# Attention output with tokens on partitions: exponentials as the stationary operand, 65 moving columns

## The chip, the cores and the metric

The kernel runs on one core of a Trainium2 chip. The metric is the device time of one execution in microseconds (us), the median of several runs. The engines are named as the profile names them: PE is TensorE (PEld its weight loads), ACT is ScalarE, DVE is VectorE, POOL is GpSimd, SP is SyncE, which here only issues DMA transfers.

## The reference

Attention with an exponential feature map, without softmax over keys, and then a feed-forward block with g = h cos h:

```python
def phi(x):
    proj = np.einsum('bhsd,df->bhsf', x, w_phi)
    proj = proj - np.max(np.abs(proj), axis=-1, keepdims=True)
    return np.concatenate([np.exp(proj), np.exp(-proj)], axis=-1)
q_p, k_p = (phi(q), phi(k))
kv = np.einsum('bhsf,bhsd->bhfd', k_p, v)
z = np.sum(k_p, axis=2)
num = np.einsum('bhsf,bhfd->bhsd', q_p, kv)
den = np.einsum('bhsf,bhf->bhs', q_p, z)[..., None] + 1e-06
attn = num / den
...
x = attn.transpose(0, 2, 1, 3).reshape(B * S, H * D)
h = x @ w_in
out = (h * np.cos(h)) @ w_out
```

There are 8 batches of 8 heads, 576 tokens (S), 64 columns a head (D), 128 features (256 after phi). The feed-forward block takes 4608 tokens, 512 columns in, 2048 hidden, 512 out. All is float32.

## The kernel before

**Attention** works in 32 units u, each a batch and a pair of heads (j = 0, 1). A unit loads q and k with head columns on partitions (qr, kr) and v with tokens on partitions (vmain, vtail, with a 65th column of ones). PE projects them (q_mm, k_mm), DVE takes the largest absolute value, it is subtracted, and ACT takes exponentials: ek with tokens on partitions, eq with features on partitions, `[128, 2, 576]` for each head, one half for each sign. kv_mm (line 666) multiplies ek by v: for each of 4 token slots, 2 heads, 2 signs and 2 halves of 64 features, 64 stationary columns of ek against the 65 moving columns of v. So one PSUM bank holds kv and, in each 65th column, z. kv_out copies them to SBUF: kv (line 680) and z, repeated 32 times (line 681).

The attention output then comes with head columns on partitions and tokens moving. z_mm (line 705) forms the denominators: the 32 copies of z are stationary, 288 tokens move, 8 matmuls into four 32-row groups of one bank. n_mm (line 715) forms the numerators: 64 columns of kv stationary, 512 tokens moving, and the 64 tail tokens into the free end of the bank of z_mm. Meanwhile invert (DVE, lines 721 to 725) reduces the 32 equal rows with a transposing reduction, adds 1e-6 and takes reciprocals; spread (ACT, line 732) moves four blocks of 32 partitions; turn (DVE, line 736) repeats them over 576 columns by transposing 32-blocks; times (DVE, line 740) multiplies numerators by them, the tail first. store (SP, line 744) writes the 128 x 576 result to the scratch tensor xs in DRAM, one DMA, 2304 bytes a row.

**The feed-forward block** reads xs back as x_raw, 512 tokens (a chunk c) at a time, splits it in high and low float32r parts (x_high on ACT, x_low on DVE), and passes pairs of 128-wide hidden blocks through mm1 (line 905 for the first three chunks, line 857 in a seven-product scheme for the others), cosine, and mm2 (lines 954 to 956). Chunks 0 to 2 are visited several times (visits 0 to 8) while the weights are being converted by ACT and DVE; chunks 3 to 8 once each (visits 9 to 14) with weights reloaded from DRAM. A chunk of 512 tokens needs the four units of each batch it touches: chunk 0 units 0 to 3, chunk 1 units 0 to 7, chunk 2 units 4 to 11.

**Order.** Each piece of work is a `Step` with an engine, a planned cost, the steps it depends on, and the buffers it takes and uses. The table `ORDER` lists all steps, 3572 of them, and is the program order on each engine: engines run their steps in that order and wait on semaphores. `plan()` only gives out the 8 PSUM banks along it. The costs given to `Step` do not act at run time. SBUF buffers come in rings (`rings`: for instance rb=2, kv=2, x_raw=4). `K_SUMS` names the units in which PE subtracts the maxima of k itself (k_sub, line 610), so that ACT can take exponentials of 512 columns at once (line 619); in the other units ACT does it with a bias per 128 columns (line 622), and DVE makes the negative of the maxima (line 605).

Of the kernel before, what the change touches and what calls it, by code (L numbers as in the profile page):

```python
# [17 lines left out]
P = 128  # L18
# [7 lines left out]
def phi_attention_then_cos_ffn(ctx: ExitStack, tc: tile.TileContext, qT, kT, vS, vT, w_phi, w_in, w_out, out):  # L26
# [41 lines left out]
    class Step:  # L68
# [16 lines left out]
    SHAPE = dict(mm1="full", mm2="full", one="full", k_mm="upper", k_end="full", q_end="full", k_sub="full", kv_mm="left", n_mm="left", z_mm="quarter", q_mm="upper")  # L85
    ORDER = [
# [237 lines left out]
    def bank(b):  # L324
        return banks[b.slot]
# [26 lines left out]

    GROUP = 3
    Q_DVE = range(0)
    K_SUMS = range(8)
    WARM = 7
    WHOLE = 8  # L360
    W_POOL = ()
    PLAIN = 9
    NP = NFT // 2
    HC = CT // 2
# [123 lines left out]

    stored, quotient, chain_v = {}, {}, {}

    def attention(u):
        d = {}
# [579 lines left out]
```

## Time and profile before

| | us |
|---|---|
| runs of the kernel before | 1080.25, 1080.84, 1082.85 (median 1080.84) |
| the profiled execution | 1081.13 |
| its span, first to last instruction | 1079.0 |
| PE busy | 1061.1 |
| ACT busy | 833.2 |
| DVE busy | 781.3 |
| POOL busy | 145.2 |

A row of the profile's groups reads: line, engine, operation, output<-inputs, shapes, xcount, then busy time in all, mean ns of one, and the idle time of that engine just before them with what ended it. Matmuls are pipelined and their ends are modelled, so the cost of one in a stream is read from the distance of two starts. A float32 matmul counts as two instructions, a float32r one as one. A row of the waits reads: who waited <- for whom: total us, times, longest us.

### The profile page before, as it was taken

What the parts mean: (1) busy time and instruction counts of PE and PEld (TensorE: products, weight loads), DVE (VectorE), ACT (ScalarE), POOL (GpSimd) and SP (SyncE); (2) the same over time, 40 slices, a digit from 0 to 9 for tenths busy, and PEclk for the clock granted to TensorE, in tenths of its full rate; (3) what the DMA queues carried; (4) which work ended last, traced back from release to release, by engine and by line L of the source; (5) the groups of instructions that cost most, each with busy time, mean ns of one, the idle gap of its engine ahead of it and who ended that gap; (6) DMA issues with size and microseconds to landing.
All of it is one profiled execution on the core that took longest, in us unless ns stands there. A gap on an engine that the chain in (4) does not pass through costs nothing.

```text
span 1079.0 us, 21627 instructions
## 1 busy us (share of the span) xinstructions
PE 1061.1 (98%) x8462; PEld 850.1 (79%) x8462; DVE 781.3 (72%) x1337; ACT 833.2 (77%) x1794; POOL 145.2 (13%) x175
## 2 busy tenths in 40 slices
PE   9999999999999999999999999999999999999998
PEld 6565666778878877888877977877788888998996
DVE  6999989899989977666776657675676556455544
ACT  6999998898886789777789778898788565454533
POOL 4424222100100210101311110211101100000000
PEclk9999999999999999999999999999999999999999
DMA  7564383566656643795356563457244743761952
GB/s 236 157 195 139 125 293 116 211 240 222 219 228 248 201 171 123 244 376 198 103 180 208 198 223 127 144 213 271 108 162 160 244 148 119 259 230 43 326 207 78
DMA packets 97477, 207.51 MB, mean 192 GB/s; under 512 B 43744, under 2 KB 50016, under 8 KB 91488
## 3 DMA queue, kind: packets, MB, share of 16 engines
q1 hardware_dynamic: 97216, 206.07, 55.4%
q8 instruction: 66, 1.08, 0.4%
q14 instruction: 35, 0.29, 0.1%
q10 hardware_dynamic: 160, 0.07, 0.0%
HBM read 155.78 MB, written 50.33 MB: 191 GB/s over the span
## 4 chain that ended last, share of the span: by engine, by line
PE 81%; ACT 8%; DVE 7%; DMA 1%; issue 1%; SPq 1%; ACTq 0%; DVEq 0%
PE bank L857 21%; PE bank L954 11%; PE bank L955 11%; PE bank L956 11%; PE bank L905 10%; PE bank L715 4%; PE bank L666 4%; PE bank L705 2%; ACT ek L622 2%; PE bank L566 2%; PE bank L520 2%; ACT eq L628 1%; PE bank L672 1%; DVE mk L602 1%; PE bank L610 1%
## 5 line engine op out<-in xcount | busy, mean ns | idle before, releaser
L954 PE MATMUL bank<-wo,gh 128*128 128x512 f32 x576 | 228.7, 397 | 0.0
L955 PE MATMUL bank<-wo,gh 128*128 128x512 f32 x576 | 225.7, 392 | 0.0
L956 PE MATMUL bank<-wo,gl 128*128 128x512 f32 x576 | 224.6, 390 | 0.9 <-DVE gl L54 0.9
L869 ACT ACTIVATE hs<-bank 128x256 f32<-128x256 f32 x192 | 70.6, 384 | 97.6 <-PE bank L857 87.4
L931 DVE SCALAR_TENSOR_TENSOR g<-g,hs 128x512 f32<-128x512 int32 x144 | 102.7, 725 | 43.2 <-ACT g L927 34.3
L956 PEld LDWEIGHTS bank<-wo,gl 128*128 128x128 f32 x576 | 108.2, 188 | 25.0 <-DVE gl L54 1.3
L938 DVE TENSOR_TENSOR g<-hs,g 128x512 f32<-128x512 f32 x144 | 101.2, 709 | 36.8 <-ACT g L935 36.3
L54 DVE TENSOR_TENSOR gl<-g,gh 128x512 fp32r<-128x512 f32 x144 | 100.5, 703 | 37.8 <-ACT gh L49 37.2
L954 PEld LDWEIGHTS bank<-wo,gh 128*128 128x128 f32 x576 | 108.6, 189 | 24.3 <-issue 4.2
L559 POOL TENSOR_TENSOR pq<-pq,bq 128x576 f32<-128x576 f32 x64 | 101.4, 1604 | 178.4 <-DVE bq L555 164.4
L857 PE MATMUL bank<-xh_t,wi 128*128 128x256 f32 x768 | 124.3, 284 | 0.0
L935 ACT ACTIVATE g<-g,halfpi 128x512 f32<-128x512 f32 x144 | 101.9, 719 | 27.3 <-DVE g L931 26.6
L955 PEld LDWEIGHTS bank<-wo,gh 128*128 128x128 f32 x576 | 108.7, 189 | 17.2
L857 PEld LDWEIGHTS bank<-xh_t,wi 128*128 128x128 f32 x768 | 110.5, 190 | 11.1 <-issue 1.7
L551 POOL COPY m<-m 32x36 f32<-32x36 f32 x96 | 42.4, 441 | 530.4 <-DVE m L546 526.5
L49 ACT ACTIVATE gh<-g 128x512 fp32r<-128x512 f32 x144 | 91.1, 635 | 25.9 <-DVE g L938 14.1
L857 PE MATMUL bank<-xh_b,wi 128*128 128x256 f32 x576 | 93.4, 284 | 0.0
L905 PE MATMUL bank<-xh_b,wi 128*128 128x512 f32 x288 | 82.9, 396 | 4.5 <-ACT ek L622 3.0
L857 PEld LDWEIGHTS bank<-xh_b,wi 128*128 128x128 f32 x576 | 81.6, 191 | 6.2 <-DVE g L938 1.5
L628 ACT ACTIVATE eq<-pq 128x576 f32<-128x576 f32 x128 | 80.3, 694 | 5.3 <-PE bank L715 3.8
L857 PE MATMUL bank<-xl_t,wi 128*128 128x256 f32 x384 | 77.3, 283 | 0.0
L666 PEld LDWEIGHTS bank<-vmain,ek 128*64 128x64 f32 x2048 | 63.5, 138 | 15.4 <-issue 8.1
(98 smaller groups left out, 1928.3 us busy)
## 6 DMA issues: line engine op xcount, KB each, us to landing
wi<-wi_parts SPq DMA_DIRECT2D x30, 1792.0 KB, 8.2
wo<-wo_parts SPq DMA_DIRECT2D x30, 1024.0 KB, 6.1
wi_parts<-wi SPq DMA_DIRECT2D x8, 2048.0 KB, 9.5
x_raw<-xs SPq DMA_DIRECT2D x60, 256.0 KB, 5.0
qr<-qT SPq DMA_DIRECT2D x32, 320.0 KB, 4.9
kr<-kT SPq DMA_DIRECT2D x32, 320.0 KB, 4.9
xs<-rb SPq DMA_DIRECT2D x32, 288.0 KB, 3.2
vmain<-vS SPq DMA_DIRECT2D x32, 256.0 KB, 4.5
```

What stands on the lines that cost most here:

```text
L49: ACT.activation(out=out, in_=in_, func=AF.Copy, scale=1.0)
L54: eng.tensor_tensor(out=out, in0=in_, in1=hi.bitcast(F32), op=ALU.subtract)
L559: qeng.tensor_tensor(out=d["pq"][:, c], in0=d["pq"][:, c], in1=d["bq"][:, c], op=ALU.subtract)
L666: PE.matmul(out=acc[c:c + 64, n, i, :], lhsT=e[:, s, P * n + c:P * n + c + 64], rhs=vmain[u % 2][:, s, i, :], start=(s == 0 and i == 0 and ...
L857: PE.matmul(out=out, lhsT=w[:, part, block, j * P:(j + 1) * P], rhs=d[x, name][:, j * HC:(j + 1) * HC], start=start and k == 0, stop=k == ...
L905: PE.matmul(out=bank(b), lhsT=w[:, part, 2 * r + kt // 2, kt % 2 * P:(kt % 2 + 1) * P], rhs=d[x, BLOCKS[kt]], start=(k == 0), stop=(k == 3 ...
L931: DVE.scalar_tensor_tensor(out=g, in0=g.bitcast(I32), scalar=-TWO_PI, in1=m["hs", r], op0=ALU.mult, op1=ALU.add)
L935: ACT.activation(out=n["g"], in_=n["g"], func=AF.Sin, bias=halfpi, scale=1.0)
L938: DVE.tensor_tensor(out=n["g"], in0=m["hs", r], in1=n["g"], op=ALU.mult)
L954: PE.matmul(out=a, lhsT=gh[:, t], rhs=w[:, 0, r], start=first, stop=False)
L955: PE.matmul(out=a, lhsT=gh[:, t], rhs=w[:, 1, r], start=False, stop=False)
L956: PE.matmul(out=a, lhsT=gl[:, t], rhs=w[:, 0, r], start=False, stop=last)
```

## The change

The output is formed with tokens on partitions. x_mm takes the place of z_mm and n_mm: 64 columns (tokens) of eq are stationary, and the 65 columns of kv with z, as kv_mm left them, move. It is two steps with a bank each: 16 matmuls for token slots 0 and 1, and 16 for slots 2 and 3 with 4 for the tail. Numerators and their denominator then lie in the same row, so invert reads the 65th columns, adds 1e-6 and takes reciprocals, and times multiplies each row by its own, in pieces of 32 columns placed so that a 32-block transposition (turn, now at the end) brings head columns onto partitions. The result lies in four groups of 32 partitions, and store writes it with eight DMAs. The host permutes the columns of q to suit. kv_out is one copy of 65 columns per group, and z's copy, spread, and the 32 copies of z are gone. `K_SUMS` goes from 8 units to 7. The order table is a new one, with 3538 steps; three planned costs (w.sums, mul, kv_out) change, which act only on how such a table is made.

```diff
-    SHAPE = dict(..., kv_mm="left", n_mm="left", z_mm="quarter", q_mm="upper")
+    SHAPE = dict(..., kv_mm="left", x_mm="left", q_mm="upper")
     ORDER = [
...
-    rings.update(..., eq=3, kv=2, rb=2,
+    rings.update(..., eq=3, kv=2, rb=1, xt=2,
...
-    K_SUMS = range(8)
+    K_SUMS = range(7)
...
         def kv_out():
-            acc = d["acc"][:, 0:260].rearrange("p (g c) -> p g c", c=65)
-            kv = d["kv"] = new("kv", [P, 4, 64], F32, "kv")
-            z = d["z"] = new("kv", [P, 4, 32], F32, "z", "z")
-            ACT.activation(out=kv, in_=acc[:, :, 0:64], func=AF.Copy, scale=1.0)
-            ACT.activation(out=z, in_=acc[:, :, 64:65].broadcast_to([P, 4, 32]), func=AF.Copy, scale=1.0)
+            kv = d["kv"] = new("kv", [P, 4, 65], F32, "kv")
+            ACT.activation(out=kv, in_=d["acc"][:, 0:260].rearrange("p (g c) -> p g c", c=65), func=AF.Copy, scale=1.0)
...
+        def x_mm(i):
+            ps = d["xps", i] = bank(xb[i])
+            started = set()
+            for t in (2 * i, 2 * i + 1):
+                for j in range(2):
+                    for n in range(2):
+                        for h in range(2):
+                            c = P * t + 64 * h
+                            g = 2 * (t - 2 * i) + j
+                            PE.matmul(out=ps[64 * h:64 * h + 64, 65 * g:65 * g + 65], lhsT=d["eq", j][:, n, c:c + 64],
+                                      rhs=d["kv"][:, 2 * n + j, :], start=h not in started, stop=n == 1, skip_group_check=True)
+                            started.add(h)
+            if i == 1:
                 for n in range(2):
                     for j in range(2):
+                        PE.matmul(out=ps[64 * j:64 * j + 64, 260:325], lhsT=d["eq", j][:, n, CT:S], rhs=d["kv"][:, 2 * n + j, :],
+                                  start=False, stop=n == 1, skip_group_check=True)
 
         def invert():
+            dn = d["dn"] = new("rb", [P, 9], F32, "dn", "dn")
+            for i, (g, n) in enumerate(((0, 4), (4, 5))):
+                DVE.tensor_scalar(out=dn[:, g:g + n], in0=d["xps", i][:, 0:65 * n].rearrange("p (g c) -> p g c", c=65)[:, :, 64], scalar1=1e-6,
+                                  scalar2=None, op0=ALU.add)
+            DVE.reciprocal(out=dn, in_=dn)
+
+        def times(i):
+            if i == 0:
+                d["rb"] = new("rb", [P, S], F32, "rb")
+            n = 4 + i
+            x = d["xps", i][:, 0:65 * n].rearrange("p (g c) -> p g c", c=65)[:, :, 0:64]
+            f = d["dn"][:, 4 * i:4 * i + n].unsqueeze(2).broadcast_to([P, n, 64])
+            for t in range(2):
+                o = d["rb"][:, 0:CT].rearrange("p (j e t b) -> p t j e b", j=2, e=2, t=NSLOT)[:, 2 * i + t]
+                y, z = (v[:, 2 * t:2 * t + 2, :].rearrange("p j (e b) -> p j e b", e=2) for v in (x, f))
+                DVE.tensor_tensor(out=o, in0=y, in1=z, op=ALU.mult)
+            if i == 1:
+                DVE.tensor_tensor(out=d["rb"][:, CT:S], in0=x[:, 4], in1=f[:, 4], op=ALU.mult)
 
         def turn():
+            d["xt"] = new("xt", [P, S], F32, "xt")
+            DVE.transpose(out=d["xt"], in_=d["rb"])
 
         def store():
             bt, hp = u // NHP, u % NHP
-            SP.dma_start(out=xs[hp * P:(hp + 1) * P, bt * S:(bt + 1) * S], in_=d["rb"])
+            x = d["xt"]
+            rows = xs[hp * P:(hp + 1) * P, bt * S:(bt + 1) * S].rearrange("(q p) t -> p q t", p=32)
+            for a in range(4):
+                r = slice(32 * a, 32 * a + 32)
+                SP.dma_start(out=rows[:, :, P * a:P * a + P], in_=x[r, 0:CT].rearrange("p (q t) -> p q t", q=4))
+            for a in range(4):
+                r, j, h = slice(32 * a, 32 * a + 32), a // 2, a % 2
+                SP.dma_start(out=rows[:, 2 * j:2 * j + 2, CT + 32 * h:CT + 32 * h + 32], in_=x[r, CT:S].rearrange("p (q t) -> p q t", q=2))
+
+        xb = [Buf("bank", "a"), Buf("bank", "a")]
+        mms = []
+        for i in range(2):
+            mms.append(Step("PE", 0.94 if i == 0 else 1.18, lambda i=i: x_mm(i), [ko] + eqs, take=[xb[i]], use=[b["kv"]] + eqb, kind=phase + "x_mm"))
+        dv = Step("DVE", 0.45, invert, mms, take=[b["rb"]], use=xb, kind=phase + "invert")
+        outs = [Step("DVE", 0.4 if i == 0 else 0.5, lambda i=i: times(i), [mms[i], dv], use=[xb[i], b["rb"]], kind=phase + "times") for i in range(2)]
+        outs[1].deps.append(outs[0])
+        tn = Step("DVE", 0.69, turn, outs, take=[b["xt"]], use=[b["rb"]], kind=phase + "turn")
+        stored[u] = Step("SP", 1.6, store, [tn], use=[b["xt"]], kind=phase + "store")
...
     qT, kT = blocks(q), blocks(k)
+    w = n * P
+    qT[..., :w] = qT[..., :w].reshape(NU, 2 * D, 4, n, 32).swapaxes(2, 3).reshape(NU, 2 * D, w)
```

More of the change, by code (lines that the diff above doesn't have):

```diff
@@ L84, in phi_attention_then_cos_ffn @@
     SWITCH = dict(e=1.3, s=1.3, full=0.23, left=0.147, quarter=0.138, upper=0.195)
-    SHAPE = dict(mm1="full", mm2="full", one="full", k_mm="upper", k_end="full", q_end="full", k_sub="full", kv_mm="left", n_mm="left", z_mm="quarter", q_mm="upper")
+    SHAPE = dict(mm1="full", mm2="full", one="full", k_mm="upper", k_end="full", q_end="full", k_sub="full", kv_mm="left", x_mm="left", q_mm="upper")
     ORDER = [
[199 rows of a table removed]
[197 rows of a table added]
     ]
@@ L309, in phi_attention_then_cos_ffn @@
     ps = ctx.enter_context(tc.tile_pool(name="ps", bufs=1, space=PSUM))
-    rings.update(wi=3, wo=3, v=2, kr=2, qr=2, pq=2, bq=1, pk=4, pk_t=2, ek=2, ek_t=2, eq=3, kv=2, rb=2,
+    rings.update(wi=3, wo=3, v=2, kr=2, qr=2, pq=2, bq=1, pk=4, pk_t=2, ek=2, ek_t=2, eq=3, kv=2, rb=1, xt=2,
                  x_raw=4, hs=4, g=3, gh=3, gl=3, o=2, w_raw=1, w_t=1)
@@ L468, in convert @@
         if kind == "wi":
-            s8 = Step(name, 1.32 * slow, sums, [s4, s6], use=[t], port=True, kind="w.sums")
+            s8 = Step(name, 1.71 * slow, sums, [s4, s6], use=[t], port=True, kind="w.sums")
             s9 = Step("ACT", 0.95, sums_high, [s8], use=[t, slot], kind="w.sums_high")
@@ L485, in reload @@
         w_ready[me] = [Step("SP", 5.6 if kind == "wi" else 3.2, load, w_stored[me], take=[slot], kind="r.load")]
-    stored, quotient, chain_v = {}, {}, {}
+    stored, chain_v = {}, {}
     def attention(u):
@@ L497, in attention @@
         qname, qeng, qcost = ("DVE", DVE, 0.77) if u in Q_DVE else ("POOL", POOL, 1.5)
-        b = {k: Buf(k) for k in ("kr", "qr", "v", "pq", "bq", "kv", "rb")}
+        b = {k: Buf(k) for k in ("kr", "qr", "v", "pq", "bq", "kv", "rb", "xt")}
         def load():
@@ L691, in attention @@
                         kind=phase + "kv_mm")
-        ko = Step("ACT", 0.45, kv_out, [last], use=[acc, b["kv"]], kind=phase + "kv_out")
-        N0 = CT
-        cut = [slice(0, N0), slice(N0, S)]
-        def z_mm():
-            d["zps"] = ps = bank(zps)[:, 0:HALF]
-            d["nps", 0], d["nps", 1] = bank(nps)[:, 0:N0], bank(zps)[:, HALF:HALF + S - N0]
-            for n in range(2):
-                for hf in range(2):
-                    for j in range(2):
-                        g = 2 * j + hf
-                        PE.matmul(out=ps[32 * g:32 * g + 32], lhsT=d["z"][:, 2 * n + j, :],
-                                  rhs=d["eq", j][:, n, hf * HALF:(hf + 1) * HALF], start=(n == 0), stop=(n == 1),
-                                  skip_group_check=True)
@@ L709, in n_mm @@
-        def n_mm():
-            for hf in (1, 0):
+        ko = Step("ACT", 0.27, kv_out, [last], use=[acc, b["kv"]], kind=phase + "kv_out")
+        def x_mm(i):
[11 more added lines that the diff above has]
+            if i == 1:
@@ L713, in n_mm @@
                 for n in range(2):
                     for j in range(2):
-                        PE.matmul(out=d["nps", hf][64 * j:64 * j + 64], lhsT=d["kv"][:, 2 * n + j, :],
-                                  rhs=d["eq", j][:, n, cut[hf]], start=(n == 0 and hf == 0), stop=(n == 1),
-                                  skip_group_check=True)
+                        PE.matmul(out=ps[64 * j:64 * j + 64, 260:325], lhsT=d["eq", j][:, n, CT:S], rhs=d["kv"][:, 2 * n + j, :],
+                                  start=False, stop=n == 1, skip_group_check=True)
@@ L719, in invert @@
         def invert():
-            dn = d["dn"] = new("rb", [P, NJ], F32, "dn", "dn")
-            DVE.tensor_reduce(out=dn, in_=d["zps"].rearrange("p (j t) -> p j t", t=32), axis=AX.X, op=ALU.max,
-                              apply_transpose=True)
-            DVE.tensor_scalar(out=dn, in0=dn, scalar1=1e-6, scalar2=None, op0=ALU.add)
-            d1 = d["d1"] = new("rb", [P, 2 * NJ], F32, "d1", "d1")
-            DVE.reciprocal(out=d1.rearrange("p (h b) -> p h b", h=2), in_=dn.unsqueeze(1).broadcast_to([P, 2, NJ]))
@@ L727, in spread @@
-        def spread():
-            for q in range(4):
-                c = slice((1 - q % 2) * NJ, (2 - q % 2) * NJ)
-                r, o = 32 * q, 32 * (q ^ 1)
-                ACT.activation(out=d["d1"][r:r + 32, c], in_=d["d1"][o:o + 32, c], func=AF.Copy, scale=1.0)
-        def turn():
-            d["rb"] = new("rb", [P, S], F32, "rb")
-            DVE.transpose(out=d["rb"], in_=d["d1"].unsqueeze(2).broadcast_to([P, 2 * NJ, 32]))
-        def times(hf):
-            rb = d["rb"][:, cut[hf]]
-            DVE.tensor_tensor(out=rb, in0=d["nps", hf], in1=rb, op=ALU.mult)
+            dn = d["dn"] = new("rb", [P, 9], F32, "dn", "dn")
@@ L742, in store @@
+        def turn():
+            d["xt"] = new("xt", [P, S], F32, "xt")
+            DVE.transpose(out=d["xt"], in_=d["rb"])
         def store():
             bt, hp = u // NHP, u % NHP
-            SP.dma_start(out=xs[hp * P:(hp + 1) * P, bt * S:(bt + 1) * S], in_=d["rb"])
-        zps, nps = Buf("bank", "a"), Buf("bank", "a")
-        zm = Step("PE", 0.97, z_mm, [ko] + eqs, take=[zps], use=[b["kv"]] + eqb, kind=phase + "z_mm")
-        dv = Step("DVE", 0.9, invert, [zm], take=[b["rb"]], use=[zps], port=True, kind=phase + "invert")
@@ L749, in attention @@
-        dv = Step("ACT", 0.9, spread, [dv], use=[b["rb"]], kind=phase + "spread")
-        dv = Step("DVE", 0.7, turn, [dv], use=[b["rb"]], kind=phase + "turn")
-        mm = Step("PE", 1.94, n_mm, [zm], take=[nps], use=[zps, b["kv"]] + eqb, kind=phase + "n_mm")
-        outs = [Step("DVE", 0.61 if ps is nps else 0.14, lambda hf=hf: times(hf), [mm, dv], use=[ps, b["rb"]], kind=phase + "times") for hf, ps in ((1, zps), (0, nps))]
-        stored[u] = Step("SP", 0.9, store, outs, use=[b["rb"]], kind=phase + "store")
@@ L754, in attention @@
-        d["b"] = b["rb"]
-        quotient[u] = d
+            x = d["xt"]
[6 more added lines that the diff above has]
+                SP.dma_start(out=rows[:, 2 * j:2 * j + 2, CT + 32 * h:CT + 32 * h + 32], in_=x[r, CT:S].rearrange("p (q t) -> p q t", q=2))
@@ L859, in product, with mul @@
                             k += 1
-                def mul(bank_b, half, block, name, start, deps, cost=0.685, wi=wi, product=product):
+                def mul(bank_b, half, block, name, start, deps, cost=0.72, wi=wi, product=product):
                     return Step("PE", cost, lambda: product(bank_b, half, block, name, start), [ready[name]] + w_ready[wi] + deps,
```

396 rows, old and new, of the table ORDER are left out of this document.

## The prediction

> **What bounds the kernel now.** I read the page's head and busy table first, then the 40 slices, the idle time of TensorE (PE), stretches of the span, and last the in-stream cost of the steps that go.
>
> ```profile
> span 1079.0 us, 21627 instructions
> ...
> PE 1061.1 (98%) x8462; PEld 850.1 (79%) x8462; DVE 781.3 (72%) x1337; ACT 833.2 (77%) x1794; POOL 145.2 (13%) x175
> ...
> PEclk9999999999999999999999999999999999999999
> ```
>
> ```profile
> 0.00:30.00 30.00, 27.81 (x294) 18.07 (x294) 21.30 (x40) 21.30 (x44) 11.70 (x28) 1.00 0.68 212
> 30.00:330.00 300.00, 293.37 (x2508) 211.08 (x2506) 276.10 (x451) 270.38 (x571) 58.59 (x62) 1.00 0.58 195
> 330.00:870.00 540.00, 535.92 (x4412) 439.25 (x4411) 371.27 (x662) 436.88 (x970) 74.89 (x85) 1.00 0.57 197
> 870.00:1079.00 209.00, 204.03 (x1260) 181.69 (x1252) 112.64 (x187) 104.64 (x212) 0.00 (x0) 1.00 0.48 174
> ```
>
> The columns of the second are stretch, length, busy time of PE, PEld, DVE, ACT and POOL, granted clock, DMA share and GB/s. PE is busy 98% at full clock everywhere. From 330 us on nothing else is near: DVE has 371.27 of 540 us. But from 30 to 330 us three engines are nearly full together: PE 98%, DVE 92%, ACT 90%. So a microsecond taken off PE is worth a microsecond late, and early only as far as DVE and ACT can follow. The profiled execution took 1081.13 us, the span of 1079.0 and 2.1 us around it; the median of the runs is 1080.84, the same within its spread, so I sum against 1081.1.
>
> **PE: the two products that go, and the one that comes.** This is one unit of attention in the PE's own order of time (start, length, what; the length of the last includes the drain, so starts are what counts):
>
> ```profile
> 823.99 0.40 PE L857 MATMUL bank<-xl_b,wi 128*128 128x256 f32 x2
> 824.31 1.18 PE L705 MATMUL bank<-eq,z 128*32 128x288 f32 x16
> 825.42 2.17 PE L715 MATMUL bank<-eq,kv 128*64 128x64 f32 x16
> 827.42 2.04 PE L666 MATMUL bank<-vmain,ek 128*64 128x65 f32 x64
> 829.29 0.61 PE L672 MATMUL bank<-vtail,ek 128*64 128x130 f32 x8
> 829.83 0.50 PE L954 MATMUL bank<-wo,gh 128*128 128x512 f32 x1
> 830.17 0.39 PE L955 MATMUL bank<-wo,gh 128*128 128x512 f32 x1
> 830.40 0.40 PE L956 MATMUL bank<-wo,gl 128*128 128x512 f32 x1
> ```
>
> z_mm (L705) holds PE 825.42 - 824.31 = 1.11 us, n_mm (L715) 827.42 - 825.42 = 2.00: 3.11 us a unit go. The new product has 16 + 20 = 36 matmuls, 64 stationary columns of exponentials against 65 moving ones, alternating between the two output halves. That is the very form of kv_mm (L666), whose 32 matmuls show as 64 instructions (float32 counts twice) in 829.29 - 827.42 = 1.87 us, 29.2 ns each, weight loads included. So 72 x 29.2 ns = 2.10 us come, 1.01 less a unit, **32 x 1.01 = 32.3 us**.
>
> The clearest objection is the weight load, since the wide operand now is the stationary one.
>
> ```profile
> L666 PEld LDWEIGHTS bank<-vmain,ek 128*64 128x64 f32 x2048 | 63.5, 138 | 15.4 <-issue 8.1 <-ACT pq L531 1.4 <-ACT ek L619 1.0
> L666 PE MATMUL bank<-vmain,ek 128*64 128x65 f32 x2048 | 66.6, 223 | 0.0
> ```
>
> One load takes 138 ns, but 2048 of them occupy only 63.5 us, 31 ns each: they overlap, four at a time. I take the 29.2 ns. The Trainium skill, "TensorE: Matmul & The Clock Gate", section "LDWEIGHTS (loading the stationary operand)", prices a load by its columns alone, columns / 1.2 ns; an estimate by that page is 64 / 1.2 = 53 ns a load, 72 loads 3.8 us a unit, 0.7 us more than the 3.11 that go, 23 us slower in all. The trace disagrees with its use as a rate here: 64 loads and matmuls took 1.87 us, not 3.4.
>
> **Changes of shape.** By the order tables, neighbouring PE steps differ in stationary shape 187 times before and 152 after (the 32 visits to a 32-column shape go). At 823.99 two matmuls of 118 ns end at 824.23 and z_mm starts at 824.31, 0.08 us lost; at 829.83 the next start comes after 0.34 us instead of 0.23, 0.11 lost. 35 x 0.09 = **3.2 us** off PE (0 where a change hides behind a wait).
>
> **A wait inside the old pair.** The tail of n_mm lies in z_mm's bank, so it waits until DVE has read the sums.
>
> ```profile
> PE bank L715 <- DVE dn L721: 3.8, 6, 0.7
> PEld bank L715 <- DVE dn L721: 7.8, 7, 1.2
> ```
> ```profile
> 869.21 1.18 PE L705 MATMUL bank<-eq,z 128*32 128x288 f32 x16
> 871.00 2.17 PE L715 MATMUL bank<-eq,kv 128*64 128x64 f32 x16 [0.61 <-DVE dn L721]
> ```
>
> There 871.00 - 869.21 = 1.79 instead of 1.11, 0.68 us lost, 6 or 7 times: 4 to 5. The halves of the new product have a bank each and nothing between them waits for DVE: **4.5 us** off. Both start, as z_mm did, behind kv_out on ACT and the exponentials; that wait stays.
>
> **K_SUMS 8 to 7.** Unit 7's two maxima are no longer subtracted by PE (L610) but as a bias of ACT's exponentials (L622 in place of L619).
>
> ```profile
> L610 PE MATMUL bank<-mk,minus 128*128 128x512 f32 x32 | 16.3, 612 | 0.2 <-DVE mk L602 0.2
> L622 ACT ACTIVATE ek<-bank,mk 128x128 f32<-128x128 f32 x224 | 70.0, 429 | 0.0
> L619 ACT ACTIVATE ek<-bank 128x512 f32<-128x512 f32 x32 | 17.2, 608 | 1.5 <-PE bank L666 1.0 <-PE bank L610 0.5
> ```
>
> PE: 16.3 us over 16 steps, so two steps are **2.0 us** less. ACT: 16 x 0.43 for 4 x 0.61, 4.4 us more, once, hidden or not by the sum for ACT below.
>
> PE in all: 32.3 + 3.2 + 4.5 + 2.0 = 42.0 us less, 1039 if every microsecond counts.
>
> **DVE.** Rows of what goes, and the nearest rows of what comes:
>
> ```profile
> L721 DVE TRANSPOSE_TENSOR_REDUCE dn<-bank 128x9 f32<-128x288 f32 x32 | 15.2, 477 | 17.3 <-PE bank L705 11.2 <-PE bank L715 6.1
> L725 DVE RECIPROCAL d<-dn 128x18 f32<-128x18 f32 x32 | 8.5, 266 | 1.1
> L723 DVE TENSOR_SCALAR dn<-dn 128x9 f32<-128x9 f32 x32 | 7.9, 245 | 1.1
> L736 DVE STREAM_TRANSPOSE rb<-d 128x576 f32<-128x576 f32 x32 | 24.6, 768 | 5.7 <-ACT d L732 5.5
> L740 DVE TENSOR_TENSOR rb<-bank,rb 128x512 f32<-128x512 f32 x32 | 21.8, 681 | 1.6 <-PE bank L715 1.1
> L740 DVE TENSOR_TENSOR rb<-bank,rb 128x64 f32<-128x64 f32 x32 | 6.9, 215 | 0.5
> L888 DVE TENSOR_TENSOR hs<-bank,hs 128x256 f32<-128x256 f32 x48 | 20.3, 422 | 54.2 <-PE bank L857 43.9 <-ACT gh L49 3.6 <-ACT g L927 3.0
> ```
>
> Gone per unit: 0.477 + 0.245 + 0.266 + 0.768 + 0.681 + 0.215 = 2.65 us. Coming: two small additions from the banks (0.245 each), a reciprocal of 9 (at most 0.266), four products of 128 columns, one of 64, and a turn of 576. A product of 128 columns lies between 0.215 (64) and 0.422 (256); along that line 0.284. Sum 0.49 + 0.27 + 4 x 0.284 + 0.215 + 0.768 = 2.88, **0.23 more**, between -0.05 (four at 0.215) and +0.78 (four at 0.422, if the strided 32-column pieces are slow). That is 3 us over the 14 units of the early stretch; late it is hidden by DVE's idle third.
>
> **ACT** loses the copy of z and the four spreads:
>
> ```profile
> L732 ACT ACTIVATE d<-d 32x9 f32<-32x9 f32 x128 | 26.7, 209 | 8.6 <-DVE d L725 7.0
> L681 ACT ACTIVATE z<-bank 128x128 f32<-128x128 f32 x32 | 8.9, 280 | 0.0
> ```
>
> 4 x 0.209 + 0.280 = 1.12 us a unit, 36 us in all, 15.6 in the early stretch against the 4.4 above: ACT falls from 270 to 259 us of work there. It is off the bound late; early it is what lets PE move up.
>
> **What the early stretch gives back.** Units 1 to 14 lie between 30 and 330 us (z_mm's 224 instructions there, 16 a unit):
>
> ```profile
> 30.00:330.00 300.00, 17.18 (x224) 5.87 (x224) 1.00 0.58 195
> ```
>
> PE would save 14 x 1.11 + 2.0 + about 2 of the waits = 19.5 us there, and the stretch would last 280.5. DVE has 276.1 + 3 = 279 us to do in it, 99.6%: too much. The new table puts 357 DVE steps ahead of unit 14's product where the old has 362; five steps of some 0.7 us leave 276. Between DVE's 92% of now and 100% I take 96%, which is an estimate: 276 / 0.96 = 288, so 12.5 of the 19.5 us are got and **7 are lost**, as new idle time of PE. Ends: 0 lost, or all 19.5.
>
> **SP and DMA.** One store of 128 rows becomes eight issues, in 32-partition pieces. They go through SP's queue in order, in front of loads.
>
> ```profile
> 509.84 0.32 SPq L744 DMA_DIRECT2D xs<-rb  x1
> 510.25 0.39 SPq L785 DMA_DIRECT2D x_raw<-xs  x1
> 510.73 0.45 SPq L483 DMA_DIRECT2D wo<-wo_parts  x1
> 511.24 0.56 SPq L507 DMA_DIRECT2D vmain<-vS  x1
> ```
> ```profile
> SPq L483 <- PE bank L857: 170.7, 27, 22.8
> ...
> SPq L783 <- DMA xs<-rb: 20.1, 8, 3.8
> ```
>
> An issue takes 0.3 to 0.6 us, so eight take about 4.4 us instead of 0.33; the step's planned cost rises only from 0.9 to 1.6. Queued behind are the next units' q, k and v and the rows of the chunk (x_raw), whose reader is ACT (x_high), then PE. Late, SP itself mostly waits for PE to give up weight buffers (170.7 us, first row), so four more microseconds find room there: nothing. Early, three chunks begin on stores just made (the second row: SP waits up to 3.8 us for a store to land before it issues x_raw). If each came 4 us late, 12 us; if the loads have that lead, 0. I take **2**. The bytes are the same and the DMA share stands at 0.48 to 0.68 in the stretches above: nothing.
>
> **Sum.** 1081.1 - 42.0 + 7 + 2 = 1048.
>
> **Rivals.**
> 1. *All of PE's saving counts* because the new order fills the early stretch: 1039. For it: ACT has 11 us less to do there. Against: DVE would need 99.6%.
> 2. *The early stretch gives nothing*, since DVE, not PE, sets its end: 1081.1 - 42.0 + 19.5 = 1059; with slow strided products (+0.55 us for 14 units) up to 1066. For it: DVE 92% busy already. Against: idle 8%, and ACT, the second brake, is relieved.
> 3. *Slower: SP's queue becomes the bound.* Each store holds it 4.1 us longer. It decides from the point where a unit costs PE over 1.3 us of waiting (42.0 / 32). If units 0 to 11, whose stores the first three chunks and the next units' loads wait for, each passed the full 4.1 us on, and the early saving were gone as well: 1059 + 49 = 1108. For it: in-order queue, stores sit right ahead of loads. Against: units are some 10 to 15 us apart there.
> 4. *Slower: the weight loads run one after the other.* Alternating 64-column loads at 138 ns, 72 of them, is 9.9 us a unit, 6.8 more, in all 1081 + 218 = 1299; the point is 3.11 us / 72 = 43 ns a load. Against it stands the same form at 29.2 ns.
> 5. *No change*: gains on PE and new waits cancel, 1081.
>
> **How the numbers follow.** The forecast (1042 to 1056) has 0.48, rival 1 (1036 to 1042) 0.15, rival 2 (1056 to 1066) 0.22, something between 1066 and 1078 0.04, rival 5 0.04, rival 3 0.05, rival 4 0.02. So faster by over 0.3% (about what a measurement of this kernel can tell from no change) 0.89, within 0.04, slower 0.07. The range 1038 to 1064 leaves out rivals 3 to 5, the gap and the outer ends of 1 and 2, under 0.2.
>
> **What would show it.** After: 72 new PE instructions per unit in about 2.1 us, some 29 ns each, and no 128x288 form; PE's busy time near 1020 us, its waits for DVE's dn gone; DVE busy over 94% in the first 300 us, with new PE idle time there that names DVE or ACT; the store's eight issues over 4 us. I am wrong if the new product takes over 2.5 us a unit, if the products of 128 columns take over 0.4 us, or if PE waits long for x_raw or for q and k early.

## The result and the profile after

The changed kernel takes 1054.09 us (median; 1052.74 to 1056.54) against 1081.45 before, ratio 0.9749 with an interval of 0.9727 to 0.9771: 27 us faster. The profiled execution took 1054.31 us with a span of 1052.6. The forecast was 1048 within 1038 to 1064.

Head and busy times of the page of the changed kernel:

```profile
span 1052.6 us, 24383 instructions
...
PE 1032.3 (98%) x9738; PEld 882.6 (84%) x9738; DVE 758.5 (72%) x1435; ACT 794.7 (76%) x1640; POOL 131.0 (12%) x175
```

PE's busy time fell by 28.8 us (1061.1 to 1032.3; the prediction named "near 1020" as a sign) and its share stayed 98%: it is still the bound. The stretches (length, busy time and count of PE, PEld, DVE, ACT, POOL, granted clock, DMA share, GB/s):

```profile
0.00:30.00 30.00, 28.53 (x342) 19.96 (x344) 21.09 (x46) 21.64 (x42) 10.19 (x28) 1.00 0.70 210
30.00:330.00 300.00, 288.28 (x3087) 230.84 (x3087) 274.32 (x508) 262.76 (x522) 54.70 (x65) 0.99 0.61 196
330.00:870.00 540.00, 537.71 (x5227) 472.31 (x5226) 368.09 (x732) 421.37 (x899) 66.11 (x82) 1.00 0.60 203
```

From 30 to 330 us PE was idle 300 - 288.28 = 11.7 us; before it was 6.6. Late, 2.3 of 540; before 4.1. So late PE waits for next to nothing, and the early stretch gave something back, as forecast. But DVE is at 274 of 300 us there, 91%, not at 96%: something else held it up. One unit of the new product late, in order of time:

```profile
763.34 2.09 PE L699 MATMUL bank<-kv,eq 128*64 128x65 f32 x64
765.25 0.40 PE L705 MATMUL bank<-kv,eq 128*64 128x65 f32 x8
765.49 2.04 PE L664 MATMUL bank<-vmain,ek 128*64 128x65 f32 x64
767.35 0.61 PE L670 MATMUL bank<-vtail,ek 128*64 128x130 f32 x8
```

765.49 - 763.34 = 2.15 us for 72 instructions, 29.9 ns each, where 2.10 was forecast; kv_mm right behind it takes 1.86 for its 64, 29.1 ns. So loading the exponentials as the stationary operand adds nothing to the 29 ns that an instruction of this form takes.

The DVE rows that answer to those forecast:

```profile
L724 DVE TENSOR_TENSOR rb<-bank,dn 128x128 f32<-128x128 f32 x128 | 29.3, 279 | 0.4
L730 DVE STREAM_TRANSPOSE xt<-rb 128x576 f32<-128x576 f32 x32 | 24.7, 771 | 0.7 <-DMA xs<-xt 0.2 <-issue 0.2
L713 DVE RECIPROCAL dn<-dn 128x9 f32<-128x9 f32 x32 | 6.9, 215 | 1.1
L726 DVE TENSOR_TENSOR rb<-bank,dn 128x64 f32<-128x64 f32 x32 | 6.7, 211 | 0.0
L711 DVE TENSOR_SCALAR dn<-bank 128x5 f32<-128x5 f32 x32 | 4.9, 154 | 9.3 <-PE bank L705 5.9 <-ACT hs L865 3.4
L711 DVE TENSOR_SCALAR dn<-bank 128x4 f32<-128x4 f32 x32 | 4.8, 148 | 7.4 <-PE bank L699 7.4
```

4 x 0.279 + 0.771 + 0.215 + 0.211 + 0.154 + 0.148 = 2.62 us a unit against the 2.65 that went: DVE is not charged at all (0.23 more was forecast; the small additions and the reciprocal make most of the difference).

What does stand out is SP's queue and what waits behind it. The first fence is the queue from 61 to 70 us, the second PE's waits and the third ACT's waits for transfers, of the changed kernel (the fourth is ACT's row of the kernel before):

```profile
61.27 0.43 SPq L502 DMA_DIRECT2D kr<-kT  x1
62.49 3.73 SPq L738 DMA_DIRECT2D xs<-xt  x4
66.26 1.85 SPq L741 DMA_DIRECT2D xs<-xt  x4
68.22 0.37 SPq L501 DMA_DIRECT2D qr<-qT  x1
68.69 0.38 SPq L502 DMA_DIRECT2D kr<-kT  x1
69.15 0.39 SPq L779 DMA_DIRECT2D x_raw<-xs  x1
```
```profile
PE bank L901 <- ACT ek L620: 4.1, 3, 1.7
PE bank L564 <- DMA kr<-kT: 1.9, 1, 1.9
```
```profile
ACT xh_t L49 <- DMA x_raw<-xs: 6.9, 3, 2.4
ACT xh_b L49 <- DMA x_raw<-xs: 4.2, 2, 2.7
```
```profile
ACT xh_b L49 <- DMA x_raw<-xs: 1.0, 1, 1.0
```

One store holds SP's queue from 62.49 to 68.11, 5.6 us, and x_raw is issued behind it, at 69.15. ACT then waits 11.1 us in all for x_raw, 8.4 of them before 330 us; before, it was 1.0. ACT works in order, so what stands behind x_high waits too, and then mm1 on PE (line 901). This is the same place in the timeline of ACT and PE; between the two lines ACT computes ek until 76.63, and mm1 waits for that:

```profile
73.44 0.63 ACT L49 ACTIVATE xh_t<-x_raw 128x512 fp32r<-128x512 f32 x1 [2.28 <-DMA x_raw<-xs]
76.67 1.35 PE L901 MATMUL bank<-xh_b,wi 128*128 128x512 f32 x3 [1.58 <-ACT ek L620]
```

PE's wait for kr (line 564) is another matter: that kr was issued at 61.27, ahead of this store and behind the one before, and landed 5.9 us later. What made it late is open.

### The profile page after: what moved, and what is told of

It reads as the page before. It is cut to its first block, busy times and chain, and to the rows that moved or that the text cites. A ratio compares the mean times of both kernels' runs of the same rounds, so it can differ in the third digit from the quotient of the medians.

```text
span 1052.6 us, 24383 instructions
## 1 busy us (share of the span) xinstructions
PE 1032.3 (98%) x9738; PEld 882.6 (84%) x9738; DVE 758.5 (72%) x1435; ACT 794.7 (76%) x1640; POOL 131.0 (12%) x175
## 4 chain that ended last, share of the span: by engine, by line
PE 78%; DVE 7%; DMA 6%; ACT 5%; SPq 2%; issue 1%; POOL 0%; ACTq 0%; DVEq 0%; POOLq 0%
PE bank L853 22%; PE bank L950 11%; PE bank L951 11%; PE bank L952 11%; PE bank L901 10%; PE bank L699 3%; PE bank L664 3%; PE bank L564 2%; PE bank L518 2%; ACT ek L620 2%; DMA xs<-xt 1%; DMA x_raw<-xs 1%; DMA vmain<-vS 1%; SPq L738 1%; SPq L741 1%
## 5 line engine op out<-in xcount | busy, mean ns | idle before, releaser
L927 DVE SCALAR_TENSOR_TENSOR g<-g,hs 128x512 f32<-128x512 int32 x144 | 99.3, 697 | 54.7 <-ACT g L923 45.9
L54 DVE TENSOR_TENSOR gl<-g,gh 128x512 fp32r<-128x512 f32 x144 | 97.7, 683 | 34.7 <-ACT gh L49 33.8
L557 POOL TENSOR_TENSOR pq<-pq,bq 128x576 f32<-128x576 f32 x64 | 97.7, 1548 | 191.1 <-DVE bq L553 151.1
L549 POOL COPY m<-m 32x36 f32<-32x36 f32 x96 | 31.9, 332 | 501.7 <-DVE m L544 499.0
L620 ACT ACTIVATE ek<-bank,lk 128x128 f32<-128x128 f32 x232 | 71.4, 407 | 5.5 <-DVE lk L603 3.5
```

Of the source, the lines that this page charges most:

```text
L54: eng.tensor_tensor(out=out, in0=in_, in1=hi.bitcast(F32), op=ALU.subtract)
L557: qeng.tensor_tensor(out=d["pq"][:, c], in0=d["pq"][:, c], in1=d["bq"][:, c], op=ALU.subtract)
L620: ACT.activation(out=e[:, g, s * P:(s + 1) * P], in_=pk[:, g, :], func=AF.Exp, scale=1.0 - 2.0 * s, bias=d["lk" if s == 0 else "mk", i][:, ...
L927: DVE.scalar_tensor_tensor(out=g, in0=g.bitcast(I32), scalar=-TWO_PI, in1=m["hs", r], op0=ALU.mult, op1=ALU.add)
```

## The experiments

Differences are taken between the ratios to the kernel before, times 1082 us; the interval of a difference is put together from both (root of the sum of squares).

**What the eight stores cost.** `one_store`, the unit's result as it lies, in one DMA:

```diff
-            for a in range(4): ... SP.dma_start(out=rows[:, :, P * a:P * a + P], ...)
-            for a in range(4): ... SP.dma_start(out=rows[:, 2 * j:2 * j + 2, ...], ...)
+            SP.dma_start(out=xs[hp * P:(hp + 1) * P, bt * S:(bt + 1) * S], in_=d["xt"])
```

> The changed kernel, with the store of each unit as one DMA of 128 rows again instead of eight (the rows then land in other places than the reference has them; bytes the same). Theory A, that the eight issues in SP's queue hold up the loads of x_raw and of q and k in the first 330 us: 5 to 8 us less, 1046 to 1049. Rival B, that DVE and ACT are too full there and the queue costs nothing: 0 to 2 less, 1052 to 1054. ACT's wait for x_raw before 330 us (8.4 us in the changed kernel) should fall to about 1 either way.

Measured 1045.95 us, ratio 0.9661 (0.9641 to 0.9681): 9.5 us less than the changed kernel, give or take 3.2. That is theory A, a little above its range. No wait of ACT for x_raw is left among its waits, and in the early stretch DVE is near the share that the prediction had assumed:

```profile
30.00:330.00 300.00, 294.06 (x3144) 236.89 (x3143) 283.18 (x522) 268.91 (x534) 61.88 (x70) 1.00 0.62 204
```

DVE 283 of 300 us, 94%, PE idle 5.9 us instead of 11.7. The product of unit 14 starts at these times (first line the kernel before, second the changed kernel, third one_store):

```profile
321.66 1.18 PE L705 MATMUL bank<-eq,z 128*32 128x288 f32 x16
314.56 1.15 PE L699 MATMUL bank<-kv,eq 128*64 128x65 f32 x32
308.10 1.09 PE L699 MATMUL bank<-kv,eq 128*64 128x65 f32 x30
```

So 6.5 of the 8.4 us between the two last spans were lost before it. (The very first product starts later in one_store, at 24.1 us for 21.0; counted from there, it is 9.6 us.)

**Issue or landing?** `store_plus7`: that one store, and behind it seven DMAs of the pieces' sizes to a scratch tensor.

```diff
+            SP.dma_start(out=xs[hp * P:(hp + 1) * P, bt * S:(bt + 1) * S], in_=x)
+            rows = junk[...]  # seven pieces, nobody reads them
```

> One store of 128 rows, as in one_store, and behind it in SP's queue seven DMAs of the sizes of the changed kernel's pieces that write to a scratch tensor nobody reads (the rows of the output land in other places than the reference has them). Theory A1, that the cost of the eight pieces is the time of their issue in SP's queue, 4 us a unit ahead of the next load: as the changed kernel, 1052 to 1056. Theory A2, that it is the landing of the pieces, for which x_raw waits: as one_store, 1045 to 1048.

1056.06 us, ratio 0.9778 (0.9756 to 0.98): 12.7 us more than one_store, 3.1 more than the changed kernel, with 11.8 us of ACT waiting for x_raw again. x_raw does not depend on the seven. So it is the time of the issues in the queue, A1, and not the landing of pieces. The seven also move 224 KB a unit more (3 x 64 + 4 x 8); but x_raw itself, once issued, lands in a median of 4.5 us here, 4.7 in one_store and 4.4 in the changed kernel, so nothing shows that the fuller DMA queues slowed it.

```profile
ACT xh_t L49 <- DMA x_raw<-xs: 6.9, 3, 3.5
ACT xh_b L49 <- DMA x_raw<-xs: 4.9, 3, 2.5
```

**Four of the eight by POOL**, `store_pool_tail`:

```diff
-                SP.dma_start(out=rows[:, 2 * j:2 * j + 2, CT + 32 * h:...
+                POOL.dma_start(out=rows[:, 2 * j:2 * j + 2, CT + 32 * h:...
```

> The four small pieces of each store (the 64 tail tokens) are issued by POOL in place of SP. By A1 some half of the 9 us comes back, 1048 to 1051; if POOL's own in-order work (the subtraction of q's maxima) is held up by its wait for the transposition, or POOL takes long for an issue, 1054 or more.

1051.98 us, ratio 0.9723 (0.9703 to 0.9743): 2.8 less, with an interval of 3.2, so not told apart from nothing, and below the half that was expected. POOL is not free of it: an issue takes 0.55 us there, and it waits 86.5 us in all for the transposition (xt), with the subtraction of q's maxima queued behind. ACT's wait for x_raw is gone in this run, but in its place ACT waits 6.5 us for that subtraction (second row; 1.1 in the changed kernel): a part of the cost has moved to another in-order queue.

```profile
L741 POOL DMA_DIRECT2D xs<-xt x128 | 69.7, 550 | 87.5 <-DVE xt L730 86.5 <-issue 0.4
ACT eq L626 <- POOL pq L557: 6.5, 3, 3.4
```

**Which engine the early stretch hangs on.** Three runs add about 11 to 14 us of work to one engine in units 0 to 14, one adds it to PE late:

```diff
x0_early, x0_late   lambda i=i: [x_mm(i) for _ in range(2 if i == 0 and u < 15 else 1)]   (late: u >= 15)
turn_early          for _ in range(2 if u < 15 else 1): DVE.transpose(out=d["xt"], in_=d["rb"])
exp_early           for _ in range(2 if u < 15 and s == 1 and j == 1 else 1): ACT.activation(out=e[:, s, :], ...)
```

> The first half of the new product is done twice in units 0 to 14: 15 x 0.95 = 14.2 us more of PE work, early only. If PE still sets the pace there: 1054 + 14 = 1068. If DVE, ACT or SP do (theories A and B alike): part of it is hidden, 1058 to 1063.

> The same in units 15 to 31: 17 x 0.95 = 16.2 us more of PE work, late only. If PE sets the pace there without slack, as the prediction had it: 1070. If late PE work is partly hidden: below 1066.

> The last transposition is done twice in units 0 to 14: 15 x 0.77 = 11.6 us more of DVE work early. Theory B with DVE as the engine that is full: 1054 + 9 to 12 = 1063 to 1066. Theory A, or ACT as the full one: 1054 to 1059.

> The second exponential of one head is taken twice in units 0 to 14: 15 x 0.72 = 10.8 us more of ACT work early. If the early stretch hangs on ACT as much as on DVE (11.6 us more of DVE cost 7): 1059 to 1063. If ACT, relieved by the change, has room: 1054 to 1057.

| | added | measured | ratio (interval) | over the changed kernel |
|---|---|---|---|---|
| x0_early | 14 us of PE, early | 1060.59 us | 0.9801 (0.9776 to 0.9827) | 5.6 +- 3.7 |
| x0_late | 16 us of PE, late | 1074.26 us | 0.9931 (0.9917 to 0.9944) | 19.7 +- 2.8 |
| turn_early | 11.6 us of DVE, early | 1062.66 us | 0.9814 (0.9792 to 0.9836) | 7.0 +- 3.4 |
| exp_early | 10.8 us of ACT, early | 1056.05 us | 0.9763 (0.9746 to 0.978) | 1.5 +- 3.0 |

Late PE work is paid in full, and somewhat more: 1074 where 1070 was expected (PE is idle 6.0 us from 330 to 870 us in x0_late, 2.3 in the changed kernel). Early, the medians have PE work paid to 40% and DVE work to 60%, but with these intervals the two can't be told apart; turn_early lies between its two expectations. ACT work costs nothing that can be told from noise: ACT, which the change relieved by 1.1 us a unit, has room. So with the stores as they are, neither PE nor DVE work is shown to be paid in full early. That they take turns, with SP's queue between them, is one reading; no run shows it.

**What the new order is worth.** `old_order_2`: new product, division and stores, in the order table of before, K_SUMS 8.

```diff
-     ORDER = [ ...3538 steps, new table... ]
+     ORDER = [ ...the table of before: z_mm -> x_mm half 0, n_mm -> half 1, spread and turn left out,
+               the earlier of the two times -> invert, times 0, times 1, turn; the later left out ]
```

> The new product, division, transposition and stores in the order of the kernel before: the two halves stand where z_mm and n_mm stood, all four DVE steps where the first of the two multiplications stood, K_SUMS is 8 units again. If the gain is PE's alone and the new table only rearranges: 1053 to 1058. If the table is what puts the freed time of PE to use in the early stretch: 1060 to 1068.

1076.18 us, ratio 0.9942 (0.9928 to 0.9957): 20.9 us slower than the changed kernel, and above both expectations. Of the 27 us only 6 remain. The run has one buffer of rb, as the changed kernel: with the two of the kernel before (the form `old_order`), it needs 1 KB a partition more SBUF than there is, so that form gave no time.

```profile
30.00:330.00 300.00, 284.71 (x2958) 225.06 (x2956) 264.76 (x490) 253.32 (x500) 59.23 (x65) 0.97 0.59 193
```
```profile
PE bank L939 <- DMA wo<-wo_parts: 5.0, 1, 5.0
PE bank L507 <- ACT kv L665: 3.4, 2, 3.0
PE bank L890 <- ACT ek L609: 2.9, 1, 2.9
```

PE is idle 15.3 us early, and once 5.0 us late for a weight load that was issued at 547.81, behind a store that held the queue from 541.48 to 546.81. Part of the loss is clock: the mean granted clock of the profiled execution is 0.990, 0.997 in the changed kernel, which on 1075 us makes some 7.5 us (an estimate from these figures; the last section has what lowers it). The run bounds the table's worth from above, since four DVE steps were put in one place without search. The product makes some 31 us of PE's time free (32 times 3.11 - 2.15), but the old order cannot use most of it.

**A version without the eight issues.** `batch_chunks_2` computes the whole thing: each unit's 512 main tokens are stored as they lie (one DMA, or two of 64 rows in later units), and the load of x_raw gathers them with 512-byte runs, feature rows in the order p, q; the rows of w_in are permuted on the host to suit. A chunk is the main part of one batch, and the ninth chunk the eight tails, whose four small DMAs are issued two SP steps later.

```diff
+            if bt < GROUP:
+                SP.dma_start(out=x_early[u], in_=x[:, 0:CT])
+            else:
+                for n in range(2):
+                    SP.dma_start(out=x_late[bt, hp // 2][n, hp % 2], in_=x[64 * n:64 * n + 64, 0:CT])
...
+                        SP.dma_start(out=raw[h, n].rearrange("p (k t) -> p k t", k=4),
+                                     in_=x_late[c, h][n].rearrange("j (a p) (q t) -> (p q) (j a) t", a=2, q=4))
```

Its first form, `batch_chunks`, stored a later unit with one DMA, `out=x_late[bt][:, hp]`, an outer dimension of 2, and kept a batch in one tensor.

> The whole computation, with the scratch tensor laid out so that one DMA stores a unit's 512 main tokens as they lie and the load of x_raw puts them in order (the rows of w_in are permuted on the host to suit); a chunk is then the 512 main tokens of one batch, and the ninth chunk the tails of all eight. The four tail DMAs follow two SP steps later. Theory A1: the loads behind a store wait for one issue and not for eight, so the 9 us come back: 1044 to 1048. If the gathering loads land late (512-byte runs where 2048 or 1024 were), or the tails' issues, still in the queue, cost as much: 1050 to 1054.

1068.15 us, ratio 0.9869 (0.9847 to 0.989): 13 us slower than the changed kernel. Its early stretch was as good as that of one_store, but late ACT waited for x_raw, and SP for the store to land. The granted clock was 0.991 in the mean.

```profile
30.00:330.00 300.00, 293.41 (x3143) 236.98 (x3140) 282.91 (x519) 267.86 (x532) 58.88 (x68) 1.00 0.63 204
```
```profile
ACT xh_b L49 <- DMA x_raw<-xl: 22.9, 6, 10.9
```
```profile
SPq L797 <- DMA xl<-xt: 46.8, 6, 12.0
```

> batch_chunks with two things mended that its trace shows after 330 us: the store of a later unit was one DMA whose outer dimension is 2, its 128 rows took some 7 to 12 us to land and ACT waited 22.9 us for x_raw; it is now two DMAs of 64 rows each. And each half of a batch has a scratch tensor of its own, so that a load of x_raw waits for its two units only. If that landing was what cost batch_chunks its gain: 1044 to 1048, the wait of ACT for x_raw under 3 us. If the gathering loads are slow in themselves: above 1055.

1048.53 us, ratio 0.9688 (0.9665 to 0.9711): 6.6 us faster than the changed kernel, give or take 3.4, so faster than the changed kernel as well as the kernel before; half a microsecond above the range that was expected. Of ACT's wait for x_raw 0.7 us are left. The two mends were made together, but the traces show the landing at a place where SP issues x_raw next behind a store (first two lines batch_chunks, last two batch_chunks_2):

```profile
516.73 0.54 SPq L747 DMA_DIRECT2D xl<-xt  x1
524.62 0.38 SPq L797 DMA_DIRECT2D x_raw<-xl  x1
518.78 1.11 SPq L748 DMA_DIRECT2D xl<-xt  x2
521.09 0.39 SPq L798 DMA_DIRECT2D x_raw<-xl  x1
```

From the issue of the store to that of x_raw it is 7.9 us in the first and 2.3 in the second. What the separate tensors add was not run by itself.

## Why the prediction was right, point by point

- *PE, the product.* Right in kind and size: 29.9 ns an instruction for 29.2, 2.15 us a unit for 2.10, so 32 x 0.96 = 30.7 us for 32.3. Rival 4, weight loads one after the other, is out.
- *The wait inside the pair*, 4.5 us: gone. No row of PE's waits names dn.
- *K_SUMS*, 2.0 us, and *changes of shape*, 3.2: not isolated by a run. With the product these work terms make 37.5 us of PE's busy time; 28.8 went (1032.3 us; 1031.6 in one_store). So the sign "near 1020" was missed by 12 us, and in the total of the page's busy time these two terms do not show.
- *DVE per unit.* 0.23 us more was forecast, none came; the products of 128 columns took 0.279 us for 0.284. What that is worth in time was not run.
- *The early stretch gives back 7 us.* The size holds where the stores are left out of it: with one store the time is 1046, which is what the sum gives without its SP term (1081.1 - 42.0 + 7 = 1046). The starts of unit 14's product split this: 13.6 us are won ahead of it and 21.2 behind it (spans of 1079.0 and 1044.2 us), where the terms say 19.5 - 7 = 12.5 and 42.0 - 19.5 = 22.5. That the sum fits better than its two parts is luck. (About 1 us of the 13.6 is no gain: one step of q that was ahead of this product now stands behind it.) The manner is only half right: DVE is at 94%, near the 96% that were taken, but the loss was to show as new idle time of PE, and in one_store PE is idle 5.9 us early for 6.6 before. The page counts the loss, like the missing busy time above, as PE being busy; matmul ends are modelled, so short waits can hide there. That DVE sets the early limit is argued, not shown: no run adds DVE work to one_store.
- *SP*, the mis-sized term: "If each came 4 us late, 12 us; if the loads have that lead, 0. I take 2." The measured cost is 9.5, near the end of no lead. The issue time was about right (4.4 forecast, 5.6 in the stretch shown); the lead of x_raw was guessed. The rows shown already spoke against a lead: SP waited up to 3.8 us for a store to land before it issued x_raw, eight times. Late the term was nothing, and about 2 us came: 19.3 us are won behind unit 14's product, 21.2 with one store. One late store spans the queue from 372.69 to 385.54 us, and PE is still idle only 2.3 of 540 us.
- *Rival 1* (1039) fell: even with one store it is 1046. *Rival 2* (1059) named the right stretch, but the early gain is not gone, 13.6 us with one store and 7.1 with eight. *Rival 3* had the right queue, with a fifth of its price (9.5 of 49). That only the stores just ahead of a chunk's load are waited for would explain the fifth; it was not tested.

That the forecast of 1048 missed by 6 us is thus in the main one term: 1046 plus 9.5 is 1055.5, and 1054 was measured. The time lies within the range because that range left room for such a miss.

## What to carry to other kernels

A product whose moving side is short can be turned round when a form of the same shape already runs in the kernel: its start-to-start time there is the price, load included. Count DMA issues like instructions: eight pieces in place of one were 4 to 6 us of an in-order queue in the first stores here (53.22 to 57.14 and 62.49 to 68.11 us), and what matters is the load that stands behind them and the in-order engine that reads it. And time taken off the bounding engine may need a new order of the work to be got: here, with the old order, 6 of 27 us were.

## What the runs showed of the hardware

**Idle time of PE can cost clock.** After the 1.87 us wait at 65 us and the idle time that follows, the changed kernel's granted clock fell (columns as above; the last two lines cut the second stretch finer):

```profile
60.00:70.00 10.00, 8.13 (x160) 6.24 (x158) 9.13 (x17) 7.87 (x15) 2.79 (x2) 1.00 0.49 144
70.00:80.00 10.00, 7.97 (x119) 6.11 (x116) 8.14 (x16) 7.72 (x25) 0.00 (x0) 0.85 1.04 333
73.70:77.10 3.40, 1.37 (x14) 0.88 (x9) 3.15 (x7) 3.40 (x13) 0.00 (x0) 0.99 0.89 292
77.10:80.50 3.40, 3.40 (x10) 2.62 (x9) 1.86 (x3) 3.40 (x11) 0.00 (x0) 0.51 1.14 420
```

0.85 over 10 us is 1.5 us of PE time, a part of what the eight stores cost. In one_store, with PE busy 8.79 and 9.51 us in the same two stretches, it stayed 1.00. In store_plus7 PE was busy 0.04 us from 126.0 to 128.5, and from 128.5 to 132.0 the clock was 0.51. In old_order_2 PE waited 2.99, 2.91 and 2.45 us up to 74.7, 106.3 and 186.4, and the clock was 0.75 from 70 to 80, 0.57 from 105 to 113 and 0.79 from 187 to 195. Not every such wait has this effect: behind one of 2.00 us at 827.9 in x0_late the clock stayed 1.00. The Trainium skill, "TensorE: Matmul & The Clock Gate", section "Part 1: The HAM clock gate (the "warmup" mystery)", says that the clock drops to half after an idle window of some 3.4 us; half speed for 3.4 of 10 us would be an average of 0.83 (an estimate by that page). The trace agrees in the drop, 0.85, and in its length, 0.51 over 3.4 us. It differs in the idle window: PE was busy 1.37 of the 3.4 us before the drop, and the clock fell all the same.

**A store with an outer dimension of 2 landed late.** The stores of batch_chunks, 256 KB with an outer dimension of 2, made SP wait up to 12.0 us for their landing. As two DMAs of 128 KB with an outer dimension of 64 each, in batch_chunks_2, they let the load behind them go after 2.3 us at the place shown above, for 7.9. Over the whole run these land in a median of 5.1 us:

```profile
xl<-xt SPq DMA_DIRECT2D x40, 128.0 KB, 5.1
```

The Trainium skill, "DMA: Bandwidth & Descriptors", section "Why a DMA increments its semaphore by 16 and not by 1", says that a DMA is split over as many engines, up to 16, as divide the outermost dimension of both its sides, so the store of batch_chunks would run on 2 (an estimate by that page). The waits agree with it; but one DMA also became two, and a run that changed the dimension alone was not made.
